# Routing logits of an attention-then-experts kernel: transposing the attention output on TensorE in fp32 instead of by DMA from DRAM in fp16

## The chip, the cores and the metric

The kernel runs on one core of one Trainium2 chip. The metric is device microseconds of that core, from the first to the last instruction and what lies around them, taken over whole executions; lower is better. The profile is one execution of the same program with the hardware profiler on.

## The reference: what is computed

Eight batches of eight heads go through attention (576 tokens, 64 columns a head). Four heads see a local band of 32 keys, four see the keys at a stride of 32. The output is laid out as 4608 tokens by 512 columns, and each token goes to one of eight experts, chosen greedily by the gate logits with a capacity of 576 tokens an expert.

```python
scores = scale * np.matmul(q, k.transpose(0, 1, 3, 2))
scores = np.where(masks[None, :, :, :], scores, -1000000000.0)
attn = softmax(scores)                       # 1e-09 added to the sum
x = np.matmul(attn, v).transpose(0, 2, 1, 3).reshape(B * S, H * D)
logits = x @ w_gate                          # 4608 x 8
...                                          # greedy assignment, cap tokens an expert
out[mask] = np.maximum(x[mask] @ w1[e], 0.0) @ w2[e]
```

The routing compares logits exactly, so the gates have to be as good as fp32.

## The kernel before, in words

**Units, pairs and steps.** The attention stage works on 16 units: for each batch `b` first its four strided heads (unit 2b, names with an `s`: `qs`, `ks`, `v_s`, `xs`), then its four local heads (unit 2b+1, names with an `l`). A unit is done in two pairs of heads, so there are 32 pairs, and a loop over steps `i` runs them in a pipeline that is written out by hand (`tc.manual_schedule()`): each engine takes its instructions in the order of the code, and none is moved. In step `i` stand, in this order, the second half of the scores of pair i+1 (`close_scores`: `dots` at L349, then the maximum on VectorE, L353), the first half of `mix` of pair i (L393, probabilities by values), the work of `mids`, the maximum of pair i+1 turned by TensorE and reduced (`max_t`, L359 to L367, ending in the tile `dd`), the second half of `mix`, the opening of the scores of pair i+2 (`masks` at L338 and the first `dots`), `norm` of pair i (L408 to L411, which writes the attention output `x` to SBUF), and `shift` of pair i+1 (L372 on TensorE, then the exponential on ScalarE, L376, which writes `pr`). Behind it come the fillers of that step (`fills`): the squares of the values on ScalarE (L288, for a common scale of each batch), `finish` (L423 on ScalarE and L424 on GpSimd split the fp32 output into two fp16 halves), `store` (DMAs to the scratch tensor `x_scr` in DRAM, L436 to L441) and `turn`. A batch is four steps.

**Memory.** The scores of a pair lie in a tile `spa` of two PSUM banks, of which there are two; `spb` is a tile of one bank, two again; `po` takes the two banks that are left. SyncE's queue issues, in the order of the code, the loads of `q`, `k` and `v` three units ahead, the stores, and the transposes; GpSimd's queue takes a part of the stores.

**The gates of before.** The two fp16 halves of a unit's output are read back from `x_scr` by a DMA that transposes them (`turn`, L446), two of these a batch. `gates` (L461) multiplies them with the gate weights, which `gate_weights`, `gate_scales` and `gate_parts` have split into two scaled fp16 halves as well (`wgh`): 16 fp16 matmuls a batch, each 32 columns wide, four side by side in the array, into 128 partial rows. ScalarE copies them to SBUF with the scale (`lt`, L464), and `logits` (L509) adds the partial rows and turns them to tokens with `sum_g`, five fp32 matmuls for each of the two layouts of a batch. Of the last batch, the local unit is turned on TensorE (`turn_last`, L477), split by ScalarE and VectorE (L485, L486), and `last_part` (L492) uses the output itself as stationary operand, 40 fp16 matmuls.

**Behind the attention.** VectorE takes the maximum of the logits, the routing search starts (L774), and the experts' stage follows: matmuls L1155 and L1203 with weights loaded and split as it goes. Nothing there is touched.

Shared helpers that the steps below rely on:

```python
def pair(i):
    return (todo[i // 2], i % 2) if 0 <= i <= last else None
def room(x):
    x[0].room(x[1])             # a new tile spa for the scores of this pair
    return x[0].sp[x[1]]
```

Of the kernel before, what the change touches and what calls it, by code (L numbers as in the profile page):

```python
# [21 lines left out]
STR = 32  # L22
# [110 lines left out]
def band_stride_attention_then_capacity_moe(ctx, tc, qt, kl, ks, nl, ns, wg, w1, w2, cst, out, dbg=None):  # L133
# [64 lines left out]
    def total(ss, po):  # L198
        nc.tensor.matmul(po, twos, ss, start=True, stop=True, skip_group_check=True)

# [19 lines left out]
    with tc.tile_pool(name="ld", bufs=2) as ld, \  # L220
# [24 lines left out]
        sg = None  # L245
        wgh = const.tile([128, H // 2, 4, E], F16, name="wgh")
        nc.vector.memset(wgh[:, :, 2:], 0.0)

        sqw = const.tile([128, 1], F32, name="sqw")
        jkw = wk.tile([128, H // 2, E], F16, name="jkw")  # L250

        def gate_weights(po):
            total(sqw, po[:, 0:1])
            nc.vector.tensor_copy(sqw, po[:, 0:1])

        def gate_scales():
            nonlocal sg
            sg, _ = scale_of(sqw, V_BITS, const)

        def gate_parts():  # L260
            nc.scalar.activation(wgh[:, :, 0], wg_sb, AF.Copy, scale=sg[:, 0:1])
            nc.vector.scalar_tensor_tensor(wgh[:, :, 1], wg_sb, sg[:, 0:1], wgh[:, :, 0], op0=OP.mult,
                                           op1=OP.subtract)

        class Unit:
# [177 lines left out]
            def turn(u):  # L443
                j = 1 if u.strided else 0
                u.xt = wk.tile([128, 2, 2, S], F16, name="xt" + u.g)
                nc.sync.dma_start_transpose(u.xt.rearrange("p a d n -> p (a d) n"), x_scr[u.b * S:(u.b + 1) * S, j])  # L446

        HB = S // 2
        ltb, gs = {}, {}

        def gate_scale(b):
            gs[b] = wk.tile([128, 1], F32, name="st")
            nc.vector.tensor_scalar(gs[b], vscale[b][0][:, 1:2], sg[:, 1:2], None, op0=OP.mult)

        def gates(b, po):
            lt = ltb[b] = wk.tile([128, S], F32, name="lt")
            xts = (todo[2 * b + 1].xt, todo[2 * b].xt)
            for a in range(2):
                for j in range(2):
                    for k in range(4):  # L460
                        nc.tensor.matmul(po[32 * k:32 * k + 32, j, :HB], wgh[:, k].rearrange("p a e -> p (a e)"),  # L461
                                         xts[k // 2][:, a, k % 2, j * HB:(j + 1) * HB],
                                         start=(a == 0), stop=(a == 1), skip_group_check=True)
            nc.scalar.activation(lt.rearrange("e (j n) -> e j n", j=2), po[:, :, :HB], AF.Copy, scale=gs[b])  # L464

        last_x = {}
# [4 lines left out]
        def turn_last(d, h, pt):  # L471
            u = todo[-1]
            j0, j1 = u.slots(parts[h])
            for j in range(j0, j1):
                n = min(128, S - 128 * j)
                x = u.x[:n, j, 2 * d:2 * d + 2].rearrange("q h d -> q (h d)")
                nc.tensor.transpose(pt[h][:, 128 * (j - j0):128 * (j - j0) + n], x, ident[:n, :n])  # L477
            if h == 0:
                last_x[d] = wk.tile([128, 2, S], F16, name=f"xtl{d}", bufs=1)

        def part_last(d, h, pt):
            c = span_l[h]
            n = c.stop - c.start
            xh, xl = (last_x[d][:, a, c] for a in range(2))
            nc.scalar.activation(xh, pt[h][:, :n], AF.Copy)  # L485
            nc.vector.scalar_tensor_tensor(xl, pt[h][:, :n], 1.0, xh, op0=OP.mult, op1=OP.subtract)  # L486

        def last_part(po, j, d):
            for a in range(2):
                for k, (r, _, tok) in enumerate(spans(B - 1)):  # L490
                    x = todo[2 * B - 2].xt[:, a, d, tok] if j else last_x[d][:, a, tok]
                    nc.tensor.matmul(po[r, k, :E * (2 - a)], x, wgh[:, 2 * j + d, :2 - a].rearrange("p a e -> p (a e)"),  # L492
                                     start=(j == 0 and d == 0 and k == 0 and a == 0), stop=(j == 1 and d == 1),
                                     skip_group_check=True)

        def last_gates(po):
            st = gs[B - 1]
            part = wk.tile([TP, 5, E], F32, name="lpart")
            sp = spans(B - 1)
            for r, c, k in ((sp[0][0], sp[0][1], slice(0, 4)), (sp[4][0], sp[4][1], slice(4, 5))):  # L500
                n = k.stop - k.start
                nc.vector.tensor_scalar(part[r, k], po[r, k, E:], st[r], None, op0=OP.mult)
                nc.vector.scalar_tensor_tensor(L[r, c:c + n], po[r, k, :E], st[r], part[r, k], op0=OP.mult, op1=OP.add)
# [26 lines left out]
        drips, late = {GW_AT + 1: [gate_scales]}, {GW_AT + 1: [gate_parts]}  # L530

        mids2, mids3 = {1: todo[1]}, {GW_AT: [lambda a, b: gate_weights(b)]}
        mids = {}

        for j, u in enumerate(todo):
# [16 lines left out]
            if not u.strided and u.b < B - 1:  # L552
                at(2 * j + (4 if u.b < B - 2 else 3), lambda k=u.b: gate_scale(k))
                if u.b < B - 2:
                    mids.setdefault(2 * j + (7 if u.b < B_LATE else G5), []).append(lambda a, b, k=u.b: gates(k, a))
                (mids if u.b == B - 2 else mids3).setdefault(2 * j + (L_AT if u.b < B_LATE else G5 + 1 if u.b < B - 2 else 5), []).append(lambda a, b, k=u.b: logits(k, b))
# [3 lines left out]
            if u is not todo[-1]:  # L560
                at(2 * j + (4 if j < 2 * B_LATE else 3 if j < nu - 2 else 1), u.turn)
# [14 lines left out]
        def pair(i):  # L576
            return (todo[i // 2], i % 2) if 0 <= i <= last else None
# [27 lines left out]
        for i in range(-1, 2 * nu):  # L605
# [17 lines left out]
            if i < last:  # L623
                for f in mids.get(i, []):
                    f(a, b)
            if i == last:
                gate_scale(B - 1)
# [15 lines left out]
            if i == last - 1:  # L643
                gates(B - 2, ps_a.tile([128, 2, 512], F32, name="spa"))
# [19 lines left out]
            if i == 0:  # L664
                nc.scalar.activation(jkw, wg_sb, AF.Square, accum_out=sqw)
            for f in late.get(i, []) + fills.get(i, []):
                f()
        po = ps_b.tile([128, 512], F32, name="spb")[:, :5 * 2 * E].rearrange("q (c e) -> q c e", e=2 * E)
# [10 lines left out]
        last_part(po, 0, 0)  # L679
        for h in range(2):  # L680
            part_last(1, h, pt)
        for f in summit(2, edge, (B - 1) * S // TP):
            f()
        for f in fills.get(last, []):
            f()
        last_part(po, 0, 1)
        for d in range(2):
            last_part(po, 1, d)
# [638 lines left out]
```

## Time and profile before

| what | value |
|---|---|
| time, median of 3 runs (lowest, highest) | 738.61 us (734.17, 739.92) |
| the profiled execution | 732.86 us, span 731.1 us |
| TensorE busy, all of the span | 622.4 us, 85% |
| VectorE, ScalarE, GpSimd busy | 456.3, 320.2, 154.1 us |
| attention, up to the last logits | 0 to 241 us |
| mean granted TensorE clock | 0.871 |

In the profile's slices, one digit is the tenths of a fortieth of the span. Rows of the timeline give the start, the duration, the engine, the source line, the operation with the tiles it writes and reads, and in brackets the idle time of the engine before it with what ended that. PE is TensorE, PEld its loading of stationary operands, DVE VectorE, ACT ScalarE, POOL GpSimd, SPq the issue queue of SyncE. "issue" in the brackets says that the profile shows nothing that was waited for. A tile written as `128*54 128x54` has 128 rows by 54 columns of stationary operand first and the moving operand behind it.

### The profile page before, as it was taken

The page shows a single profiled execution, that of the slowest core. Times are in us where ns is not written, and L with a number is a line of the kernel's source. Part 1 is how long each engine was busy: PE and PEld are TensorE (multiplying, and loading weights), DVE is VectorE, ACT ScalarE, POOL GpSimd, SP SyncE. Part 2 cuts the span into 40 slices and gives each one's busy share as a digit, 9 for nine tenths or more (in the row PEclk, how much of TensorE's full clock was granted, in tenths as well). Part 3 has the DMA queues.
Part 4 walks back from the last instruction along what each step waited for, and adds up shares of the span by engine and source line. Part 5 has one row for each costly group of instructions (what it writes and reads, how often), then busy time and mean ns, then how long its engine had stood idle before and what let it go on. Part 6 is the DMA issues. An engine that isn't in the chain of part 4 may idle for free.

```text
span 731.1 us, 19141 instructions
## 1 busy us (share of the span) xinstructions
PE 622.4 (85%) x8043; PEld 410.6 (56%) x8043; DVE 456.3 (62%) x1368; ACT 320.2 (44%) x497; POOL 154.1 (21%) x152
## 2 busy tenths in 40 slices
PE   6878886875889348999999997998998997999993
PEld 3656664654667326645845743754754753665741
DVE  3686666754787777887677674776766763652200
ACT  3444334435252024757166273356347345853210
POOL 2043223133133011032032032015005014212011
PEclk8575657878696557999999998999999999999998
DMA  9989999799764145076076087067068069561010
GB/s 217 247 244 251 215 237 202 210 238 173 212 133 97 36 159 160 1 281 146 1 281 144 1 288 139 1 229 183 16 218 207 1 222 254 211 114 51 1 37 29
DMA packets 106873, 111.23 MB, mean 152 GB/s; under 512 B 75644, under 2 KB 83414, under 8 KB 106275
## 3 DMA queue, kind: packets, MB, share of 16 engines
q1 hardware_dynamic: 98707, 88.46, 47.4%
q0 software_dynamic: 7360, 21.15, 9.5%
q8 instruction: 63, 1.03, 0.6%
q10 hardware_dynamic: 720, 0.39, 0.2%
q14 instruction: 23, 0.19, 0.1%
HBM read 73.60 MB, written 18.87 MB: 126 GB/s over the span
## 4 chain that ended last, share of the span: by engine, by line
PE 21%; DMA 14%; issue 13%; DVE 8%; SPq 4%; ACT 2%; POOL 2%; POOLq 0%; ACTq 0%; DVEq 0%
PE ph L1155 16%; DMA w<-in_w_dram 8%; DMA xg<-x_scr,idx 3%; SPq L1071 3%; PE ph L1203 3%; DMA xt<-xg 2%; DVE w2l L1017 2%; SPq L983 1%; POOL out_dram L1214 1%; ACT jk L998 1%; DVE hl L1163 1%; POOL xg L1068 1%; DVE cm L774 1%; ACT yl L1210 0%; DVE y L1211 0%
## 5 line engine op out<-in xcount | busy, mean ns | idle before, releaser
L1155 PE MATMUL ph<-xt,w1h 128*128 128x288 f16 (+2 forms) x1024 | 179.8, 291 | 13.0 <-DMA xt<-xg 9.4
L1155 PEld LDWEIGHTS <-w1h 128*128 128x128 f16 x1024 | 98.6, 99 | 44.2 <-issue 9.2
L1214 POOL DMA_INDIRECT out_dram<-y,idx x40 | 43.6, 1091 | 342.2 <-ACT y L1213 314.4
L1155 PE MATMUL ph<-xt,w1l 128*128 128x288 f16 (+2 forms) x512 | 113.9, 292 | 0.0
L998 ACT ACTIVATE jk<-w 128x1024 f16<-128x1024 f32 x64 | 67.5, 1054 | 75.1 <-DMA w<-in_w_dram 73.2
L1203 PE MATMUL ph<-w2h,hh 128*128 128x512 f16 x256 | 97.0, 379 | 0.0
L1203 PE MATMUL ph<-w2h,hl 128*128 128x512 f16 x256 | 97.0, 379 | 0.0
L1203 PE MATMUL ph<-w2l,hh 128*128 128x512 f16 x256 | 97.0, 379 | 0.0
L1162 ACT ACTIVATE hh<-ph 128x576 f16<-128x576 f32 (+2 forms) x72 | 42.9, 596 | 120.3 <-PE ph L1155 117.6
L1203 PEld LDWEIGHTS <-hh 128*128 128x128 f16 x512 | 48.4, 98 | 59.6 <-issue 9.7
L1163 DVE SCALAR_TENSOR_TENSOR hl<-ph,hh 128x576 f16<-128x576 f32 (+2 forms) x72 | 49.5, 688 | 42.2 <-ACT hh L1162 41.9
L376 ACT ACTIVATE pr<-spa 128x576 f32<-128x576 f32 x32 | 20.8, 650 | 110.3 <-PE spa L372 92.9
L1155 PEld LDWEIGHTS <-w1l 128*128 128x128 f16 x512 | 50.6, 100 | 13.8 <-issue 0.8
L424 POOL TENSOR_TENSOR xos<-xs,xos 118x768 f16<-118x768 f32 x16 | 26.7, 1672 | 122.8 <-ACT xos L423 122.8
L1068 POOL DMA_INDIRECT xg<-x_scr,idx x40 | 41.6, 1039 | 49.0 <-issue 34.7
L1017 DVE SCALAR_TENSOR_TENSOR w1l<-w,w_sw,w1h 128x512 f16<-128x512 f32 x64 | 45.8, 747 | 9.1 <-ACT w1h L1016 3.9
L1017 DVE SCALAR_TENSOR_TENSOR w2l<-w,w_sw,w2h 128x512 f16<-128x512 f32 x64 | 45.8, 745 | 7.9 <-ACT w2h L1016 7.8
L393 PE MATMUL po<-v_s,pr 64*54 64x65 f32 (+1 forms) x768 | 42.7, 268 | 7.2 <-issue 4.7
L1213 ACT ACTIVATE y<-ph,so 128x512 f32<-128x512 f32 x32 | 21.9, 683 | 57.4 <-PE ph L1203 37.8
L1016 ACT ACTIVATE w1h<-w,w_sw 128x512 f16<-128x512 f32 x64 | 41.7, 709 | 3.2 <-DVE ss_e L203 1.8
L1016 ACT ACTIVATE w2h<-w,w_sw 128x512 f16<-128x512 f32 x64 | 41.1, 710 | 3.7 <-DVE w_sw L208 3.6
L1203 PEld LDWEIGHTS <-hl 128*128 128x128 f16 x256 | 25.0, 98 | 29.4 <-issue 3.6
(613 smaller groups left out, 972.6 us busy)
## 6 DMA issues: line engine op xcount, KB each, us to landing
w<-in_w_dram SPq DMA_DIRECT2D x64, 512.0 KB
v_s<-in_ns_dram SPq DMA_DIRECT2D x16, 329.1 KB
kl<-in_kl_dram SPq DMA_DIRECT2D x8, 608.0 KB
v_l<-in_nl_dram SPq DMA_DIRECT2D x16, 292.5 KB
ql<-in_qt_dram SPq DMA_DIRECT2D x8, 576.0 KB
x_scr<-xol SPq DMA_DIRECT2D x8, 512.0 KB
ks<-in_ks_dram SPq DMA_DIRECT2D x7, 576.0 KB
qs<-in_qt_dram SPq DMA_DIRECT2D x7, 576.0 KB
```

What stands on the lines that cost most here:

```text
L393: nc.tensor.matmul(po[r:r + n, j - j0], pr[k, o:o + n], u.vn[k, t, 2 * p + h], start=(j == j0), stop=(j == j1 - 1), skip_group_check=True)
L424: eng.tensor_tensor(u.xo[:nr, :, 1, c], xf, u.xo[:nr, :, 0, c], op=OP.subtract)
L998: nc.scalar.activation(jk, wf[:, c * n4:(c + 1) * n4].rearrange("p c f -> p (c f)"), AF.Square, scale=1.41422, accum_out=sq[:, c:c + 1])
L1016: nc.scalar.activation(hi[:, c, f], wf[:, c, f], AF.Copy, scale=s_)
L1017: nc.vector.scalar_tensor_tensor(lo[:, c, f], wf[:, c, f], s_, hi[:, c, f], op0=OP.mult, op1=OP.subtract)
L1068: nc.gpsimd.indirect_dma_start(out=xg[:n], out_offset=None, in_=x_rows, in_offset=bass.IndirectOffsetOnAxis(ap=idx[:n, t:t + 1], axis=0))
L1071: nc.sync.dma_start_transpose(xt[:, :, t * 128:t * 128 + n], xg[:n])
L1155: nc.tensor.matmul(tile_[:, j, :w], wt[:, d, f * 128:(f + 1) * 128], xt[:, d // 2, xx, d % 2, c], start=(k == 0), stop=(k == 3 * DC - 1))
L1162: nc.scalar.activation(hv, src, AF.Relu)
L1163: nc.vector.scalar_tensor_tensor(lv, src, 0.0, hv, op0=OP.max, op1=OP.subtract)
L1203: nc.tensor.matmul(py, a[:, f, ts_], w[:, f], start=(k == 0), stop=(k == len(todo) - 1))
L1214: st = nc.gpsimd.indirect_dma_start(out=out_rows, out_offset=bass.IndirectOffsetOnAxis(ap=idx[:n, t:t + 1], axis=0), in_=y[:n], in_offset= ...
```

## The change

No DMA transposes are left in the attention. Each pair's output, which lies in SBUF in fp32, is transposed on TensorE one step after it was made (`turn(p, po)`): 12 transposes of a strided pair, 6 of a local one. They are written into the PSUM tile `a` that the scores of pair i+2 will take later in the same step, and ScalarE copies them to SBUF (`keep`) before those scores are opened. The first strided pair has its own path (`turn_first`, at the end of step 2). The gate weights stay in fp32, padded to 32 columns with zeros (`wgp`), and `gates(b, j)` is called twice a batch, as a filler of two successive steps: four fp32 matmuls each, of 288 columns, side by side in the array. The strided half of `lt` is written in the order of the tokens, by an activation of its own. The scales of the gate weights and their three functions go. Of the last batch, `last_strided` and `last_part` do the same in fp32, with 15 matmuls in place of 40. `finish` and `store` stay, because the experts read `x_scr`.

```diff
-            def turn(u):
-                j = 1 if u.strided else 0
-                u.xt = wk.tile([128, 2, 2, S], F16, name="xt" + u.g)
-                nc.sync.dma_start_transpose(u.xt.rearrange("p a d n -> p (a d) n"), x_scr[u.b * S:(u.b + 1) * S, j])
+            def turn(u, p, po):
+                if u.b not in xtb:
+                    xtb[u.b] = wk.tile([128, H // 2, S], F32, name="xt")
+                for j, c, t, r in u.pieces():
+                    x = u.x[r, t, 2 * p:2 * p + 2].rearrange("q h d -> q (h d)")
+                    nc.tensor.transpose(po[:, j, c:c + r.stop - r.start], x, ident[r, r])
+
+            def pieces(u):
+                if u.strided:
+                    return [(f, SQ * t, t, slice(64 * f, 64 * f + u.wide(t))) for t in range(u.nt) for f in range(2)]
+                return [(0, EV + 128 * j, j, slice(0, 128)) for j in range(3)] + \
+                    [(1, 128 * (j - 2), j, slice(0, min(128, S - 128 * j))) for j in range(2, u.nx)]
+
+            def keep(u, p, po):
+                o = 0 if u.strided else EV
+                nc.scalar.activation(xtb[u.b][:, 2 * u.strided + p].rearrange("d (j n) -> d j n", j=2), po[:, :, o:o + HB],
+                                     AF.Copy)
...
-        def gates(b, po):
-            lt = ltb[b] = wk.tile([128, S], F32, name="lt")
-            xts = (todo[2 * b + 1].xt, todo[2 * b].xt)
-            for a in range(2):
-                for j in range(2):
-                    for k in range(4):
-                        nc.tensor.matmul(po[32 * k:32 * k + 32, j, :HB], wgh[:, k].rearrange("p a e -> p (a e)"),
-                                         xts[k // 2][:, a, k % 2, j * HB:(j + 1) * HB],
-                                         start=(a == 0), stop=(a == 1), skip_group_check=True)
-            nc.scalar.activation(lt.rearrange("e (j n) -> e j n", j=2), po[:, :, :HB], AF.Copy, scale=gs[b])
+        def lt_parts(lt, po, sc, js):
+            for j, c in js:
+                nc.scalar.activation(lt[64:].rearrange("e (a r) -> e a r", r=STR)[:, :, 16 * j:16 * j + 16],
+                                     po[64:, c].rearrange("e (r a) -> e a r", a=NA), AF.Copy, scale=sc)
+
+        def gates(b, j):
+            if j == 0:
+                ltb[b] = wk.tile([128, S], F32, name="lt")
+            lt, c = ltb[b], slice(64, 64 + HB)
+            po = ps_b.tile([128, 512], F32, name="spb")
+            for k in range(4):
+                nc.tensor.matmul(po[32 * k:32 * k + 32, c], wgp[:, k], xtb[b][:, k, j * HB:(j + 1) * HB], start=True,
+                                 stop=True, skip_group_check=True)
+            sc = vscale[b][0][:, 1:2]
+            nc.scalar.activation(lt[:64, j * HB:(j + 1) * HB], po[:64, c], AF.Copy, scale=sc[:64])
+            lt_parts(lt, po, sc[64:], [(j, c)])
...
             if not u.strided and u.b < B - 1:
-                at(2 * j + (4 if u.b < B - 2 else 3), lambda k=u.b: gate_scale(k))
-                if u.b < B - 2:
-                    mids.setdefault(2 * j + (7 if u.b < B_LATE else G5), []).append(lambda a, b, k=u.b: gates(k, a))
+                for h in range(2):
+                    at(2 * j + 3 + h, lambda k=u.b, h=h: gates(k, h))
...
-            if u is not todo[-1]:
-                at(2 * j + (4 if j < 2 * B_LATE else 3 if j < nu - 2 else 1), u.turn)
...
                 for f in mids.get(i, []):
                     f(a, b)
+                if i > 1:
+                    x = pair(i - 1)
+                    po = a if m else ps_a.tile([128, 2, 512], F32, name="spa")
+                    x[0].turn(x[1], po)
+                    x[0].keep(x[1], po)
             if i == last:
-                gate_scale(B - 1)
+                last_strided()
...
-            if i == last - 1:
-                gates(B - 2, ps_a.tile([128, 2, 512], F32, name="spa"))
...
+            if i == 2:
+                for j in range(2):
+                    todo[0].turn_first(j)
```

**The order on TensorE.** One step of a middle batch on PE, from the last `dots` of the next pair to the `masks` of the one behind it (`mix` of a strided unit is L393 here, `max_t` L359), before:

```order
L349 MATMUL spa<-qs,ks 54x54 x16
L349 MATMUL spa<-qs,ks 18x18 x4
L393 MATMUL po<-v_s_129,pr 54x65 x10
L393 MATMUL po<-v_s_129,pr 18x65 x2
L359 MATMUL spa<-ident,mx_s_131 32x64 x4
L393 MATMUL po<-v_s_129,pr 54x65 x10
L393 MATMUL po<-v_s_129,pr 18x65 x2
L338 LDWEIGHTS ident_b
L338 MATMUL spa<-mask_l,ident_b 128x288
```

The same step in the changed kernel, whose lines are numbered 20 lower up to here (L329 is the `dots`, L373 `mix`, L339 `max_t`, L318 the `masks`; L428 is the new transpose):

```order
L329 MATMUL spa<-qs,ks 54x54 x16
L329 MATMUL spa<-qs,ks 18x18 x4
L373 MATMUL po<-v_s_129,pr 54x65 x10
L373 MATMUL po<-v_s_129,pr 18x65 x2
L428 MATMUL spa<-ident,xl 128x128 x5
L428 MATMUL spa<-ident,xl 128x64
L339 MATMUL spa<-ident,mx_s_131 32x64 x4
L373 MATMUL po<-v_s_129,pr 54x65 x10
L373 MATMUL po<-v_s_129,pr 18x65 x2
L318 LDWEIGHTS ident_b
L318 MATMUL spa<-mask_l,ident_b 128x288
```

The transposes of the pair before (a local one, `xl`) stand between the first half of `mix` and `max_t`; the `masks` write the tile that the transposes went into.

**The order on ScalarE.** Two steps of a middle batch on ACT before, from one exponential to the third (`jk` are the squares of the values, `xos` and `xol` are `finish`):

```order
L376 ACTIVATE pr<-spa 128x576
L288 ACTIVATE jk,vsq_115<-v_l_141 32x2304
L423 ACTIVATE xos<-xs 118x6x128
L376 ACTIVATE pr<-spa 128x576
L288 ACTIVATE jk,vsq_115<-v_l_141 32x2304
L423 ACTIVATE xol<-xl 128x5x128
L376 ACTIVATE pr<-spa 128x576
```

The first of them in the changed kernel, to the next exponential (L438 is `keep`, L467 and L455 write `lt`, L356 is the exponential, L268 the squares, L403 `finish`):

```order
L356 ACTIVATE pr<-spa 128x576
L268 ACTIVATE jk,vsq_115<-v_l_141 32x2304
L467 ACTIVATE lt<-spb,ss_s 64x288
L455 ACTIVATE lt<-spb,ss_s 64x18x16
L403 ACTIVATE xos<-xs 118x6x128
L438 ACTIVATE xt<-spa 128x576
L356 ACTIVATE pr<-spa 128x576
```

Between two exponentials now stand `keep` in every step and the two `lt` activations in two steps of four.

**The order on SyncE.** A batch's worth of the SP queue before; the changed kernel has the same rows without the two marked DMA_TRANSPOSE, and nothing else of the queue moves:

```order
L446 DMA_TRANSPOSE xts<-x_scr 128x4x576
L440 DMA x_scr<-xol 128x4x512
L441 DMA x_scr<-xol 64x512
L319 DMA v_s_133<-in_ns_dram 54x1560 x2
L312 DMA ks<-in_ks_dram 128x1152
L313 DMA qs<-in_qt_dram 128x1152
L446 DMA_TRANSPOSE xtl<-x_scr 128x4x576
L436 DMA x_scr<-xos 18x6x512
```

Each transpose stands behind loads of later units and ahead of stores and loads that the queue issues in turn.

More of the change, by code (lines that the diff above doesn't have):

```diff
@@ L243, in band_stride_attention_then_capacity_moe @@
                 vbuf[g, i] = t
[L245 to L263, printed above, removed]
+        wgp = const.tile([128, H // 2, 32], F32, name="wgp")
+        nc.vector.memset(wgp, 0.0)
         class Unit:
@@ new lines, in keep, with turn_first @@
+            def keep(u, p, po):
+                o = 0 if u.strided else EV
+                nc.scalar.activation(xtb[u.b][:, 2 * u.strided + p].rearrange("d (j n) -> d j n", j=2), po[:, :, o:o + HB],
+                                     AF.Copy)
+            def turn_first(u, j):
+                po = ps_b.tile([128, 512], F32, name="spb")
+                for f, c, t, r in u.pieces():
+                    if f == j:
+                        nc.tensor.transpose(po[:, c:c + r.stop - r.start], u.x[r, t, :2].rearrange("q h d -> q (h d)"),
+                                            ident[r, r])
+                nc.scalar.activation(xtb[u.b][:, 2, j * HB:(j + 1) * HB], po[:, :HB], AF.Copy)
@@ L488, in last_part @@
[L488 to L493, printed above, removed]
+            x = xtb[B - 1][:, d, c]
+            if h == 0:
+                nc.scalar.activation(x, pt[h][:, :c.stop - c.start], AF.Copy)
+            else:
+                nc.vector.tensor_copy(x, pt[h][:, :c.stop - c.start])
@@ new lines, in last_strided @@
+        def last_strided():
+            lt = ltb[B - 1] = wk.tile([128, S], F32, name="lt")
+            po = ps_a.tile([128, 2, 512], F32, name="spa")
+            for j in range(2):
+                for k in range(2, 4):
+                    nc.tensor.matmul(po[32 * k:32 * k + 32, j, :HB], wgp[:, k], xtb[B - 1][:, k, j * HB:(j + 1) * HB],
+                                     start=True, stop=True, skip_group_check=True)
+            for j in range(2):
+                lt_parts(lt, po[:, j], 1.0, [(j, slice(0, HB))])
@@ L494, in last_part @@
+        def last_part(po, k, first):
+            for n, (r, _, tok) in enumerate(spans(B - 1)):
+                if k is None:
+                    nc.tensor.matmul(po[r, n], ltb[B - 1][64:, tok], sum_g[64:], start=False, stop=False,
+                                     skip_group_check=True)
+                else:
+                    nc.tensor.matmul(po[r, n], xtb[B - 1][:, k, tok], wgp[:, k, :E], start=(first and n == 0), stop=(k == 1),
                                      skip_group_check=True)
@@ L496, in last_gates @@
         def last_gates(po):
-            st = gs[B - 1]
-            part = wk.tile([TP, 5, E], F32, name="lpart")
+            st = vscale[B - 1][0][:, 1:2]
             sp = spans(B - 1)
@@ L663, in band_stride_attention_then_capacity_moe @@
                 todo[1].square_v(i + 1)
-            if i == 0:
-                nc.scalar.activation(jkw, wg_sb, AF.Square, accum_out=sqw)
+            if i == 2:
+                for j in range(2):
+                    todo[0].turn_first(j)
             for f in late.get(i, []) + fills.get(i, []):
                 f()
-        po = ps_b.tile([128, 512], F32, name="spb")[:, :5 * 2 * E].rearrange("q (c e) -> q c e", e=2 * E)
+        po = ps_b.tile([128, 512], F32, name="spb")[:, :5 * E].rearrange("q (c e) -> q c e", e=E)
         turn_last(0, 0, pt)
@@ L685, in band_stride_attention_then_capacity_moe @@
             f()
-        last_part(po, 0, 1)
-        for d in range(2):
-            last_part(po, 1, d)
+        last_part(po, 1, False)
         last_gates(po)
```

28 lines of the change are left out of this document (9 added, 19 removed).

## The prediction

> **What bounds the kernel now.** The change touches only the attention, so I cut the span there by batches: windows of four steps, from one exponential (L376) to the fourth behind it, in the view that gives each engine's busy time, the granted TensorE clock, the DMA share and the rate by window.
>
> ```profile
> 29.40:58.50 29.10, 21.79 (x540) 15.72 (x538) 24.00 (x60) 11.91 (x15) 9.90 (x8) 0.70 0.90 260
> 58.50:86.40 27.90, 23.07 (x550) 16.53 (x554) 18.00 (x48) 12.27 (x16) 8.19 (x7) 0.68 0.98 233
> 86.40:114.20 27.80, 24.56 (x564) 18.52 (x565) 18.59 (x48) 12.17 (x15) 8.12 (x7) 0.65 0.96 224
> 114.20:142.30 28.10, 20.50 (x568) 15.35 (x572) 18.07 (x49) 12.21 (x16) 7.92 (x7) 0.76 0.89 210
> 142.30:172.00 29.70, 22.75 (x568) 16.36 (x563) 17.75 (x49) 12.14 (x16) 8.20 (x7) 0.77 0.95 206
> 172.00:201.80 29.80, 21.46 (x568) 15.72 (x564) 18.16 (x51) 12.16 (x16) 7.93 (x7) 0.77 0.85 203
> 201.80:225.40 23.60, 21.17 (x573) 15.98 (x570) 20.54 (x54) 10.93 (x13) 8.35 (x7) 0.86 0.63 128
> ```
>
> The columns behind the length are PE, PEld, DVE, ACT, POOL, then clock, DMA share and GB/s. Five middle batches take 27.9 + 27.8 + 28.1 + 29.7 + 29.8 = 143.3 us, 28.7 each. DMA is 85 to 98% busy in them, TensorE 72 to 88%. The batch behind them has the same work on TensorE, but the last load was issued before it and DMA is at 63%: 23.6 us.
>
> ```profile
> 190.96 1.38 SPq L313 DMA_DIRECT2D ql<-in_qt_dram  x1
> ```
>
> So a middle batch loses some 5 us to the DMAs. The list of waits in these five batches says how:
>
> ```profile
> PE spa L349 <- issue: 12.7, 3, 6.4
> PE spa L359 <- issue: 6.0, 2, 3.8
> PE spa L372 <- DVE dd L367: 4.4, 4, 1.3
> PE po L393 <- issue: 3.6, 3, 2.0
> PE spa L461 <- issue: 2.1, 1, 2.1
> ```
>
> 12.7 + 6.0 + 3.6 + 2.1 = 24.4 us of TensorE's idle time have no releaser that the profile shows. No data is missing: in the timeline the pause falls inside a run of like matmuls. The longest two:
>
> ```profile
> 113.83 8.98 SPq L446 DMA_TRANSPOSE xtl<-x_scr  x1
> 119.16 0.65 ACT L376 ACTIVATE pr<-spa 128x576 f32<-128x576 f32 x1 [1.16 <-PE spa L372]
> 124.82 0.45 PE L349 MATMUL spa<-qs,ks 64*54 64x54 f32 x8 [5.70 <-issue]
> ...
> 172.24 9.34 SPq L446 DMA_TRANSPOSE xtl<-x_scr  x1
> 183.97 0.26 PE L349 MATMUL spa<-qs,ks 64*18 64x18 f32 x6 [6.41 <-issue]
> ```
>
> They end 2.0 and 2.4 us after the transpose has left the SP queue (122.81 and 181.58). The DMA queues by window, first while the transpose is being moved (113.9 to 122.2 us), then at its end (122.2 to 124.8):
>
> ```profile
> q1 hardware_dynamic: 1223, 1.86, 102.5%
> ```
>
> ```profile
> q8 instruction: 1, 0.02, 2.5%
> ```
>
> A 16 KB block of instructions comes through only when the transpose is over. I read the pauses as TensorE out of instructions, whose fetch stands behind the transposes in the DMA engines. [...]
>
> **The change part by part.** *Removed:* 15 DMA transposes, two a batch; with them, by my reading, most of the 24.4 us.
>
> *Added on TensorE:* the transposes of 30 pairs, one pair a step. The prices, from the timeline at full clock:
>
> ```profile
> 234.33 0.86 PE L477 MATMUL spa<-ident,xl 128*128 128x128 f32 x5
> 235.12 0.44 PE L477 MATMUL po<-ident,xl 128*128 128x128 f32 x2
> ...
> 110.64 1.00 PE L393 MATMUL po<-v_s,pr 64*54 64x65 f32 x24
> ...
> 233.13 1.27 PE L509 MATMUL spb<-sum_g,lt 128*128 128x8 f32 x10
> ...
> 115.96 0.32 PE L359 MATMUL spa<-ident,mx_l 128*32 128x64 f32 x8
> ...
> 229.24 0.30 PE L461 MATMUL spa<-xtl,wgh 128*32 128x288 f16 x2
> 229.62 0.29 PE L461 MATMUL spa<-xts,wgh 128*32 128x288 f16 x2
> ```
>
> A local pair: five such transposes stand 0.79 us from the next group (234.33 to 235.12), one more makes 0.90. A strided pair has 12 of 54 rows by 128 columns, which no row shows: as cheap as `mix`, which also alternates between the two halves of the rows, 12 x 1.00/24 = 0.5; as dear as L509, which loads 128 fp32 columns each time, 12 x 1.27/10 = 1.5. I take 0.9, near the middle, since it shares one trait with each. A batch: 4 x 0.9 = 3.6 us. The fp32 gates: eight matmuls of 288 columns, four side by side. L359 ran eight of 64 columns, also in fours, in 0.32, of which about 0.2 is one matmul's own way; the second four thus cost 0.1, or 0.46 for 288 columns; two calls with their starts 1.1 (not side by side, it would be 3.7). The 16 fp16 matmuls that go took 0.67 (229.24 to 229.91). Net +0.4, so 4.0 us a batch at full clock, 4.0/0.86 = 4.7 at the clock of the undisturbed batch.
>
> *Added on ScalarE:* `keep` in each step, two pairs of `lt` activations, less one `lt`.
>
> ```profile
> L464 ACT ACTIVATE lt<-spa,st x7: 731/741/742, 80.2 to 230.0; 128x576 f32<-128x576 f32 x7
> L288 ACT ACTIVATE jk<-v_l x16: 2118/2121/2124, 16.3 to 207.4; 32x2304 f16<-32x2304 f32 x16
> L423 ACT ACTIVATE xos<-xs x16: 826/838/844, 40.5 to 226.0; 118x768 f16<-118x768 f32 x16
> ```
>
> ```profile
> 234.81 0.44 ACT L485 ACTIVATE xtl<-spa 128x320 f16<-128x320 f32 x1 [2.94 <-PE spa L477]
> ```
>
> `keep` has the shape of L464, 0.74; the `lt` pieces are a little shorter than L485, 0.4 each. ScalarE is free for more than half of a batch (12.2 of 28), but `keep` is waited for: the `masks` write the tile that it reads, and behind them stand on TensorE the opening `dots`, the second `shift` and with it the next exponential. In the two steps of a batch with local squares the queue is 0.65 + 2.12 + 0.18 + 0.8 + 0.84 + 0.74 = 5.3 us from an exponential to the end of `keep`, and masks, dots and shift about 1.5 more: 6.9 us a step. The step I forecast is 28.7/4 = 7.2, so the wait is mostly covered; at full clock it shows. I put 0.7 us a batch, between none and 2.
>
> *Given back:* the wait for `dd` (4.4 us in five batches) is on VectorE, which is behind with copies; a turn now stands ahead of `max_t` and fills it: -0.9 a batch. *Left:* fetches behind plain loads, 0.6 a batch, an estimate from the short pauses in the list.
>
> *The sum.* A middle batch: 23.6 + 4.7 + 0.7 - 0.9 + 0.6 = 28.7, five of them 143.5 against 143.3: +0.2. The batch of 201.8 to 225.4 has no pause to win back: +4.7 - 0.9 = +3.8. The window 29.4 to 58.5 lies almost wholly before the first transposes (53.6 on): four turns, the first unit's own and less weight work, 4.1/0.70 = 5.9, less a wait that hides 3.0 of it:
>
> ```profile
> L446 SPq DMA_TRANSPOSE xts<-x_scr x8: 2139/4069/6582, 53.6 to 233.9; - x8
> ```
>
> ```profile
> 50.77 0.64 PE L372 MATMUL spa<-dd,sel 128*128 128x288 bf16 x2 [2.99 <-DVE dd L367]
> ```
>
> That is +2.9. At the end:
>
> ```profile
> 236.24 1.60 PE L492 MATMUL spb<-wgh,xtl 128*128 128x16 f16 x20 [0.68 <-ACT xtl L485]
> 238.44 1.48 PE L492 MATMUL spb<-wgh,xts 128*128 128x16 f16 x20 [0.59 <-DMA xts<-x_scr]
> 240.78 0.23 DVE L503 SCALAR_TENSOR_TENSOR L<-spb,st,lpart 64x8 f32<-64x8 f32 x1
> ```
>
> Of 40 matmuls, 15 of 0.127 stay, and only five of them behind the last copies, which no longer follow each other on ScalarE and VectorE: the last transposes end at 235.6 (235.12 + 0.44), a copy 0.5, five matmuls 0.6, two writes of the logits 0.5, some 0.3 between them: near 237.5, not 241.0, -3.5; one more turn and `last_strided` cost (0.9 + 1.1 - 0.1)/0.8 = +2.3. Together -1.2. In all +0.2 + 3.8 + 2.9 - 1.2 = **+5.7 us**. The experts' stage keeps its order and shifts. The profiled execution took 732.86 us (span 731.1), so 738.6; the median of the runs, 738.61, is 5.75 above it, and on that the forecast is 744.3 us, 0.8% more. A measurement of this kernel can tell about 1% from no change.
>
> **The rivals.** *The clock stays low (slower).* I priced the added work at 0.86; in the middle batches it was granted at 0.65 to 0.77. Busy time by clock gives 15.7, 16.0, 15.6, 17.5 and 16.5 us of work a batch at full clock, 16.3 in the mean; with 4.0, at 0.73, 27.8 us, and with the idle of the last batch (23.6 - 21.2 = 2.4) and 0.4 more 30.6: +9.7 in place of +0.2, and +5 in place of +3.8: 755. For it: 86.4 to 114.2 has short pauses and still 0.65. Against: the pauses of 4 to 6 us fall into half-clock stretches. A stretch with ten transposes ran at full clock, the next at half:
>
> ```profile
> 232.29:235.71 3.42, 3.27 (x42) 2.43 (x31) 2.33 (x9) 0.44 (x1) 1.47 (x4) 1.00 0.14 37
> 235.71:239.12 3.41, 2.25 (x30) 1.87 (x30) 2.89 (x8) 1.61 (x4) 1.40 (x1) 0.50 0.72 163
> ```
>
> [...]
>
> *ScalarE's loop decides (slower).* If `keep` ends 1.5 us late in both steps with local squares, each batch pays 3.0 and not 0.7: +11.5, 756. It decides once TensorE's step is under 6.9 us.
>
> *The clock rises (faster).* Without pauses TensorE may be near full clock: at 0.92 the work is 22.1, and ScalarE's loop then sets two steps of four: 2 x 6.9 + 2 x (22.1 + 2.4)/4 = 26.0 a batch, -13.5, and -1.8 in the batch behind: 729.
>
> *The pauses are not the transposes'.* The loads share the engines; then the 24.4 us stay, each middle batch pays 4.7 + 0.7 - 0.9 = 4.5, +22.5 in place of +0.2: 767. Against it: the pauses end with the transposes. That transposes remain is excluded by the order of SP.
>
> **How the numbers follow.** The forecast, 744, own range 738 to 751: 0.35. Clock low, 755: 0.22. ScalarE, 756: 0.12. Pauses stay, 767: 0.06. Clock rises, 729: 0.25. Faster by over 1% is the last, 0.25; within 1% the forecast, 0.35; slower 0.40. From 724 to 762 leaves out most of the fourth and the far ends of the clock cases, under 0.2.
>
> **What would show it.** Right: DMA share near 0.7 in the middle batches, TensorE's pauses without releaser under 5 us in all, L428 at 0.9 us a turn, middle batches of 28 to 29 us, the batch behind them 27 to 28, logits done 3 us sooner after the last exponential. Wrong: pauses of 4 us that remain; L428 over 1.5 a strided turn; `masks` waiting for `keep` over 1 us in most steps; a mean clock under 0.7 or over 0.9 up to 225 us.

## The result and the profile after

The changed kernel takes 747.05 us (median of 19 runs, 737.89 to 754.43), the kernel before 736.48 us (19 runs, 726.58 to 741.58): ratio 1.0151, 95% interval 1.0112 to 1.0190. In this ratio and those below, executions over 1.5% above the fastest of their kernel are left out; the medians hold all. The profiled execution took 744.54 us with a span of 742.8, against 732.86 and 731.1. The forecast was 744.3 us, 0.8% slower: the side was right and the time lies in the stated range, though the change of +10.6 us is nearly twice the +5.7 forecast. The place was wrong: the forecast put its 5.7 us into the attention, and the profile has none there.

The windows of four steps for the kernel after, from exponential (now L356) to exponential, cut as in the prediction (columns: length, PE, PEld, DVE, ACT, POOL, clock, DMA share, GB/s):

```profile
30.90:64.50 33.60, 27.40 (x582) 20.59 (x586) 22.85 (x54) 15.27 (x21) 9.86 (x8) 0.70 0.73 215
64.50:91.60 27.10, 22.44 (x596) 16.09 (x597) 19.92 (x48) 16.02 (x22) 7.95 (x7) 0.94 0.65 184
91.60:117.90 26.30, 22.35 (x596) 16.22 (x598) 20.08 (x48) 16.06 (x22) 8.12 (x7) 0.94 0.66 187
117.90:147.20 29.30, 23.21 (x596) 16.64 (x597) 19.74 (x48) 16.02 (x23) 7.94 (x7) 0.88 0.60 169
147.20:173.10 25.90, 21.96 (x596) 15.58 (x592) 19.03 (x48) 15.91 (x22) 8.25 (x7) 0.93 0.68 190
173.10:199.40 26.30, 22.41 (x596) 16.52 (x598) 20.40 (x49) 16.05 (x23) 7.94 (x7) 0.94 0.63 180
199.40:224.50 25.10, 20.58 (x596) 15.17 (x592) 20.51 (x52) 14.53 (x20) 7.95 (x7) 1.00 0.18 50
```

The five middle batches take 134.9 us in place of 143.3, though TensorE has more to do: the granted clock is 0.88 to 0.94 where it was 0.65 to 0.77, and DMA is busy for two thirds of the time and not for nearly all. Busy time by clock is 20.8 us a batch at full clock (21.1, 21.0, 20.4, 20.4, 21.1) against 16.3 before: 4.5 more, where the prediction added 4.0. What TensorE waits for in these five batches (64.5 to 199.4 us; columns: total us, times, longest):

```profile
PE spa L318 <- ACT xt L438: 11.3, 9, 1.9
PE spa L352 <- DVE dd L347: 6.8, 9, 1.0
PE spa L329 <- issue: 3.1, 3, 2.6
PE po L373 <- ACT pr L356: 0.7, 4, 0.2
PE spb L519 <- issue: 0.6, 1, 0.6
```

Pauses without a releaser are 3.7 us in place of 24.4. In their stead `masks` (L318) wait for `keep` (L438). One step of ScalarE's queue shows why, with the `masks` behind it:

```profile
98.31 0.65 ACT L356 ACTIVATE pr<-spa 128x576 f32<-128x576 f32 x1 [1.20 <-PE spa L352]
...
98.98 2.12 ACT L268 ACTIVATE jk<-v_l 32x2304 f16<-32x2304 f32 x1
...
101.22 0.50 ACT L467 ACTIVATE lt<-spb,ss_s 64x288 f32<-64x288 f32 x1
...
101.73 0.50 ACT L455 ACTIVATE lt<-spb,ss_s 64x288 f32<-64x288 f32 x1
...
102.25 0.74 ACT L403 ACTIVATE xol<-xl 128x640 f16<-128x640 f32 x1
...
103.01 0.65 ACT L438 ACTIVATE xt<-spa 128x576 f32<-128x576 f32 x1
...
103.71 0.41 PE L318 MATMUL spa<-mask_s,ident_b 128*128 128x288 bf16 x2 [0.34 <-ACT xt L438]
```

From the exponential to the end of `keep` it is 103.66 - 98.31 = 5.35 us, the 5.3 of the prediction.

Over the whole attention the gain of the middle is given back at its edges. From the first exponential's window to the start of the search: start +1.5 (third exponential at 30.91, before at 29.37), first window +4.5, middle -8.4, the batch behind +1.6, last step and logits +0.5. The search starts at 245.35 us; before it started at 245.67. **In this pair of executions all 11.7 us of the span arise behind it**, where the change touches no line. (A profile is one execution, and the attention of the changed kernel is not always this short: in the profiles of two runs below, `after_less32` and `after_again`, the search starts at 253.0 and 254.8 us. What the attention costs is therefore taken from the cuts and ratios below.) First the kernel before from the search to the end, its window, its longest wait on the gathered tokens' transposes, and its queue of gathers and scatters (packets, MB, share of 16 engines):

```profile
245.70:731.10 485.40, 433.00 (x3550) 273.57 (x3550) 295.35 (x927) 220.44 (x369) 85.32 (x81) 0.94 0.44 127
```

```profile
PE ph L1155 <- DMA xt<-xg: 9.4, 6, 2.2
```

```profile
q0 software_dynamic: 5888, 18.88, 12.9%
```

The same three of the kernel after:

```profile
245.40:742.80 497.40, 436.67 (x3550) 274.62 (x3550) 295.53 (x927) 221.01 (x369) 85.61 (x81) 0.94 0.45 124
```

```profile
PE ph L1165 <- DMA xt<-xg: 15.6, 10, 2.9
```

```profile
q0 software_dynamic: 5888, 18.88, 13.5%
```

The counts of instructions, the packets and bytes of these queues and the clock are the same, but it takes 12.0 us more. The experts' hidden matmuls wait 6.2 us longer for the transposed tokens, and the same 5888 packets take 13.5% of a longer span, 67.1 us in place of 62.6 on each of 16 engines. Comparing the two built programs, one thing differs in this stage beside the DMAs' semaphore lanes and the place of the instructions in memory: every SBUF tile behind the attention lies 32 bytes a partition higher, since the new `wgp` and what it replaces do not have the same size. The first expert weights `w1` begin at byte 59616 before and 59648 after.

### The profile page after: what moved, and what is told of

The parts are those of the page before. It is cut to its first block, busy times and chain, and to the rows that moved or that the text cites. A ratio compares the mean times of both kernels' runs of the same rounds, so it can differ in the third digit from the quotient of the medians.

```text
span 742.8 us, 19700 instructions
## 1 busy us (share of the span) xinstructions
PE 634.2 (85%) x8315; PEld 416.5 (56%) x8315; DVE 464.5 (63%) x1351; ACT 348.7 (47%) x546; POOL 153.8 (21%) x152
## 4 chain that ended last, share of the span: by engine, by line
PE 19%; DMA 16%; issue 13%; DVE 6%; POOL 4%; ACT 2%; SPq 2%; POOLq 0%; ACTq 0%
PE ph L1165 17%; DMA w<-in_w_dram 8%; DMA xg<-x_scr,idx 6%; DMA xt<-xg 3%; POOL xg L1078 2%; POOL out_dram L1224 1%; DVE w2l L1027 1%; ACT jk L1008 1%; SPq L993 1%; DVE hl L1173 1%; SPq L1081 1%; DVE y L1221 0%; ACT yl L1220 0%; DVE cm L830 0%; PE ph L1066 0%
## 5 line engine op out<-in xcount | busy, mean ns | idle before, releaser
L1165 PE MATMUL ph<-xt,w1h 128*128 128x288 f16 (+2 forms) x1024 | 183.2, 296 | 19.7 <-DMA xt<-xg 15.6
L356 ACT ACTIVATE pr<-spa 128x576 f32<-128x576 f32 x32 | 20.8, 651 | 72.6 <-PE spa L352 72.6
L404 POOL TENSOR_TENSOR xos<-xs,xos 118x768 f16<-118x768 f32 x16 | 26.4, 1653 | 128.2 <-ACT xos L403 128.2
L373 PE MATMUL po<-v_s,pr 64*54 64x65 f32 (+1 forms) x768 | 35.7, 238 | 6.9 <-ACT pr L356 6.7
```

Source lines behind the costliest of these rows:

```text
L373: nc.tensor.matmul(po[r:r + n, j - j0], pr[k, o:o + n], u.vn[k, t, 2 * p + h], start=(j == j0), stop=(j == j1 - 1), skip_group_check=True)
L404: eng.tensor_tensor(u.xo[:nr, :, 1, c], xf, u.xo[:nr, :, 0, c], op=OP.subtract)
L1165: nc.tensor.matmul(tile_[:, j, :w], wt[:, d, f * 128:(f + 1) * 128], xt[:, d // 2, xx, d % 2, c], start=(k == 0), stop=(k == 3 * DC - 1))
```

## The experiments

Theory A: the cost arises in the attention, as predicted (the change pays there, the experts shift). Theory B: it arises behind the attention. Two kernels are cut behind the logits; routing and experts are left out, so what they write is not the reference's output.

```diff
+    nc.sync.dma_start(out[0:TP, 0:NC * E], L.rearrange("q c e -> q (c e)"))
+    return
```

`attn_before`:

> The kernel of before that ends behind the attention: it writes the logits into the first 128 rows of the output and leaves the routing and the experts out. Its profile before has the logits done at 241 us, so a time near 247 us. It is the base for the next one. Theory A (the change costs its 11 us in the attention, and the profiled execution was a lucky one) expects it 8 to 12 us under attn_after; theory B (the 11 us arise behind the attention) expects the two within 3 us.

`attn_after`:

> The changed kernel cut in the same way (no routing, no experts). Theory A: 255 to 259 us, 8 to 12 more than attn_before. Theory B: within 3 us of attn_before, near 246 us, since the profiled execution of the changed kernel had its last exponential at 230.0 us against 230.6.

Measured: 248.56 us (247.72 to 249.28, 4 runs) and 249.41 us (246.93, 249.28, 249.55, 271.45). The attention costs 0.9 us more by the medians, and 0.1 by the means without the run of 271.45 (248.6 against 248.5); theory A falls. For B, the address was moved alone, once in each kernel.

`before_pad32` gives the kernel before the addresses of the change behind the attention:

```diff
+        pad = const.tile([128, 8], F32, name="pad")
+        nc.vector.memset(pad, 0.0)
```

> The kernel of before with 32 bytes a partition of unused constants more, so that every tile of the routing and of the experts lies at the address that it has in the changed kernel. If the addresses of the SBUF tiles are what makes the experts' stage of the changed kernel longer: 9 to 12 us over the kernel before (1.012 to 1.016). If not: the ratio to before is within 0.4% of 1.

`after_less32` gives the changed kernel those of before:

```diff
-        warm_e = const.tile([128, 1], F32, name="warm_e")
+        warm_e = rm0[:, :1]
```

> The changed kernel with 32 bytes a partition less in front of the experts' tiles (a scratch word of the warm-up activation lies in another tile), so that these lie where they lie in the kernel before. If the addresses are the cause: within 0.4% of the kernel before. If not: 1.011 to 1.019 times the kernel before, as the changed kernel.

Measured: 739.46 us, ratio 1.0044 (0.9994 to 1.0093), and 738.85 us, ratio 1.0029 (0.9982 to 1.0077). So 32 bytes less take the changed kernel back to the kernel before, but 32 more hardly slow the kernel before, where 1.012 to 1.016 was expected of the address. To exclude that only the session had changed, the change was run again, beside a sibling 32 bytes *higher* (the two lines of `pad` ahead of `wgp`):

> The changed kernel, unaltered, measured again beside its shifted sibling. Address theory (the experts' stage is slower because all tiles behind the attention lie 32 bytes higher): 1.2 to 1.8% above the kernel before, search to end 494 to 500 us. Rival (the 10 us belonged to the first comparison or to the chip, not to the kernel): within 0.5% of before.

> The changed kernel with a constant of 32 bytes a partition more, so that the tiles behind the attention lie another 32 bytes higher: 64 above those of the kernel before, again an odd multiple of 32. Address theory, if what counts is whether a base is an odd or an even multiple of 32 bytes: within 0.5% of before, as with 32 bytes less. If any other property of the change slows the experts' stage: 1.2 to 1.8% above before, like the unaltered change.

Measured: `after_again` 749.06 us, 1.0179 (1.0127 to 1.0231); `after_plus32` 734.71 us, 0.9995 (0.9962 to 1.0028). It is not height but place: 32 bytes either way remove the loss. Next the shift was confined to what follows the attention, in both kernels:

```diff
+    pd = ctx.enter_context(tc.tile_pool(name="pd", bufs=1))
+    pad = pd.tile([128, 8], F32, name="pad")
+    nc.gpsimd.memset(pad, 0.0)
     rt = ctx.enter_context(tc.tile_pool(name="rt", bufs=2))
```

> The changed kernel with 32 bytes a partition put in between the attention and what follows: the attention's tiles stay where the change has them, only those of the routing and the experts lie 32 bytes higher. Theory that the address costs its time in the experts' stage: 0.995 to 1.006 of before, search to end 484 to 490 us. Rival that a part of it arises in the attention's own tiles: 1.006 to 1.012. Rival that it is another property: 1.015 to 1.018, 494 to 498 us.

> The kernel before with the same 32 bytes between the attention and what follows, so that the experts' tiles alone stand where the change has them. If the address is the whole cause: 1.008 to 1.018 of before, search to end 492 to 498 us. Rival (as the constant of 32 bytes in the kernel before hinted with 1.0044): 0.999 to 1.006, so the address costs its full price only together with something else that the change brings.

Measured: `after_rtpad` 740.21 us, 0.9980 (0.9935 to 1.0025): the attention's own tiles have no part in it. `before_rtpad` 741.10 us, 1.0011 (0.9966 to 1.0056): the rival holds, the address alone does not have its full price in the kernel before. All nine full kernels, sorted by where `w1` begins (the other tiles of the stage move by the same amount). The third column is from the profiled executions, search to end; then the wait of the hidden matmuls for `xt`, and the time of the 4608 packets of 4096 bytes on the queue of gathers and scatters, summed from the trace. Stage, wait and packets are of one execution each:

| kernel | `w1` at byte, rest by 256 | search to end, us | wait for `xt`, us | gather and scatter packets, engine-us | ratio to before |
|---|---|---|---|---|---|
| after | 59648, 0 | 497.4 | 15.6 | 1065 | 1.0151 |
| after_again | 59648, 0 | 495.0 | 15.9 | 1023 | 1.0179 |
| before_pad32 | 59648, 0 | 491.7 | 11.0 | 1013 | 1.0044 |
| before_rtpad | 59648, 0 | 490.4 | 11.9 | 1036 | 1.0011 |
| after_less32 | 59616, 224 | 488.8 | 7.2 | 983 | 1.0029 |
| before | 59616, 224 | 485.4 | 9.4 | 989 | 1 |
| after_rtpad | 59680, 32 | 485.2 | 4.7 | 980 | 0.9980 |
| after_plus32 | 59680, 32 | 485.0 | 11.4 | 992 | 0.9995 |
| both (below) | 59680, 32 | 481.2 | 9.2 | 966 | 1.0006 |

The row of the wait in `before_rtpad` and in `after_rtpad`, the two kernels that differ from their parents only in this:

```profile
PE ph L1158 <- DMA xt<-xg: 11.9, 8, 2.5
```

```profile
PE ph L1168 <- DMA xt<-xg: 4.7, 5, 1.6
```

All four with `w1` on a multiple of 256 have the longest stage and the slowest packets, whichever attention stands ahead; no kernel of the other five reaches them, though the nearest two are close (490.4 and 488.8 us). The three places that were tried do not tell a multiple of 256 from one of 64 or 128. In the changed kernel this is worth 11 us (496.2 against 485.1 in the mean of two and four), and the ratios say the same three times. In the kernel before it is worth 5.6 us in two profiles and 1 to 3 us in the medians of the runs, within what the intervals allow to be nothing. **That the loss is removed by moving the experts' tiles by 32 bytes is shown; why the address costs more behind the new attention is open**, as is which tile it is. At the change's addresses `w1`, the gathered tokens `xg` and their transposes `xt` all start on multiples of 256 bytes, and in the table the kernels with that place have the longer packets, 1013 to 1065 engine-us against 966 to 992. It is not the ordinary packet that differs: the median is 159 to 161 ns in all nine. Packets of more than 400 ns number 422 to 495 with `w1` on a multiple of 256 and 343 to 382 elsewhere; and the stage's 33792 packets of 256 bytes, those of the transposes, took 885 to 965 engine-us there and 811 to 880 elsewhere. What holds them up is open.

Inside the attention, three cuts test the terms of the sum. `attn_relief` is `attn_before` without its 15 DMA transposes; the gates read a tile of zeros, so the logits are left meaningless:

```diff
-                u.xt = wk.tile([128, 2, 2, S], F16, name="xt" + u.g)
-                nc.sync.dma_start_transpose(u.xt.rearrange("p a d n -> p (a d) n"), x_scr[u.b * S:(u.b + 1) * S, j])
+                u.xt = xt0
```

> The attention of the kernel before alone (cut behind the logits), without its 15 DMA transposes; the gates read a tile of zeros in their place, so the logits are not the reference's. Nothing is added on TensorE or ScalarE. Theory that TensorE's pauses come from the transposes: 222 to 228 us in place of 248.6, pauses without a releaser under 5 us in the five middle batches. Rival (the loads cause the pauses): 243 to 249.

Measured: 226.59 us (224.16 to 228.16, 4 runs), 22.0 less than `attn_before`. So the transposes cost 22 us, and the work that replaces them 249.4 - 226.6 = 22.8. (The cuts ran on three chips, on which the kernel before took 734.1 to 738.8 us; a difference of 1 to 2 us between cuts can be the chip.) Pauses without a releaser from 58 to 200 us, `attn_before` and then `attn_relief`:

```profile
PE spa L349 <- issue: 12.1, 4, 6.2
PE po L393 <- issue: 9.0, 5, 5.4
PE spa L359 <- issue: 5.8, 2, 4.7
PE spa L461 <- issue: 1.1, 1, 1.1
```

```profile
PE spa L351 <- issue: 8.1, 4, 3.7
PE po L395 <- issue: 5.8, 6, 2.8
...
PE spa L361 <- issue: 1.9, 1, 1.9
...
PE spa L462 <- issue: 0.6, 1, 0.6
```

28.0 us become 16.4, not the under 5 expected: the longest go, shorter ones stay with plain loads alone. The total was forecast well and this part of its reason was not; in the same window the granted clock rose from 0.71 to 0.84. (The windows of this cut hold more steps, since it is faster.) When the pauses end can be read from the traces: in `before`, `attn_before` and `attn_relief` each of the 18 pauses over 1.5 us in the middle batches ends 1.2 to 1.8 us after a 16 KB block has landed on the instruction queue, and the five waits of 1.9 us for `keep` in the changed kernel hold no such landing. That agrees with the prediction's reading, TensorE out of instructions; it stays a reading, since no run changes the fetch alone.

`attn_keep` moves the squares of the local values from behind the exponential to behind `keep`:

```diff
-                        at(2 * j - V_AT + f, lambda u=u, f=f: u.square_v(f), True)
+                        squares[2 * j - V_AT + f] = lambda u=u, f=f: u.square_v(f)
...
                     x[0].keep(x[1], po)
+                if i in squares:
+                    squares[i]()
```

> The attention of the changed kernel alone (cut behind the logits, routing and experts left out), with ScalarE's squares of the local values moved from behind the exponential to behind keep. Theory that the wait of masks for keep is what holds the loop (15.7 us in 12 waits): 236 to 241 us, in place of 249.4, and that wait under 4 us. Rival (the loop is held by TensorE's own work or by the DMAs, and the wait only shows slack): 246 to 250.

Measured: 246.65 us (241.39 to 257.05, 4 runs), 2.8 less and not 8 to 13; the expectation failed. The runs go with the granted clock; at like clocks the gain is 3.6 us (245.71 at 0.857 against 249.28 at 0.853) and 5.5 (241.39 at 0.879 against 246.93 at 0.877). TensorE's waits over the whole cut, `attn_after` and then `attn_keep`:

```profile
PE spa L318 <- ACT xt L438: 14.4, 11, 1.9
PE spa L352 <- DVE dd L347: 9.1, 11, 1.4
PE po L373 <- issue: 5.8, 3, 4.2
PE spa L329 <- issue: 3.3, 4, 2.1
```

```profile
PE spa L352 <- DVE dd L347: 16.7, 15, 3.3
PE spa L329 <- issue: 10.9, 6, 4.0
PE po L373 <- issue: 7.7, 4, 4.1
```

The wait for `keep` is gone, all 14.4 us, and 7.6 us of it came back as the wait for `dd`, 9.5 as pauses without a releaser. For `dd`, the timeline of `attn_keep` shows VectorE's small cast (L344) at seven times its length while GpSimd's subtraction of `finish` (L404) runs, and one without it:

```profile
141.90 1.65 POOL L404 TENSOR_TENSOR xos<-xs,xos 118x768 f16<-118x768 f32 x1 [6.32 <-ACT xos L403]
...
142.29 1.29 DVE L344 CAST mh<-mr 128x32 bf16<-128x32 f32 x1
...
157.86 0.18 DVE L344 CAST mh<-mr 128x32 bf16<-128x32 f32 x1
```

In these rows the long cast ends 0.03 us behind the subtraction (143.58 and 143.55). So do the others of this trace: 10 of its 25 casts from 59 to 225 us take over 0.8 us, and each ends 0.03 to 0.04 us behind a subtraction. The change made this worse without touching either line: the same cast from 59 to 225 us in the kernel before, and then in `attn_after` (count, busy us, mean ns):

```profile
L364 DVE CAST mh<-mr 128x32 bf16<-128x32 f32 x24 | 5.0, 208 | 0.8
```

```profile
L344 DVE CAST mh<-mr 128x32 bf16<-128x32 f32 x25 | 13.2, 529 | 0.9
```

`attn_keep2` moves `finish` behind the squares as well, out of the cast's way:

```diff
-                at(2 * j + p if j else 2, lambda u=u, p=p: u.finish(p, nc.gpsimd))
+                if 0 < j < nu - 2:
+                    fin[2 * j + p + 1] = lambda u=u, p=p: u.finish(p, nc.gpsimd)
+                else:
+                    at(2 * j + p if j else 2, lambda u=u, p=p: u.finish(p, nc.gpsimd))
...
+                if i in fin:
+                    fin[i]()
```

> The attention of the changed kernel alone, with the squares of the local values behind keep and with finish (ScalarE's copy, GpSimd's subtraction) behind both. Theory that the wait for dd, which took the place of the wait for keep (16.7 us in 15 waits), comes from VectorE's small cast L344, 0.18 us alone and 1.2 to 1.3 while GpSimd's subtraction runs: mean of L344 in 59 to 225 us from 614 to under 300 ns, that wait under 9 us, 238 to 243 us. Rival (VectorE's queue itself is late, or TensorE's pauses decide): 245 to 250 with the wait as long.

The cast in 59 to 225 us, and the waits of the cut:

```profile
L344 DVE CAST mh<-mr 128x32 bf16<-128x32 f32 x25 | 4.5, 181 | 0.9
```

```profile
PE po L373 <- issue: 8.7, 4, 5.5
PE spa L329 <- issue: 8.2, 3, 3.2
PE po L373 <- ACT pr L356: 6.3, 9, 1.1
PE spa L352 <- DVE dd L347: 5.6, 3, 3.2
```

The cast and the wait came out as expected, 181 ns and 5.6 us; the time is 245.75 us (244.19 to 247.06, 4 runs), in the rival's range and not in the 238 to 243. What is left over stands as pauses without a releaser (16.9 us) and as waits for the exponential (6.3); that TensorE, with less idle time, comes sooner to the end of its instructions and to `pr` is a reading and not tested.

Last, `both`: the whole changed kernel with 32 bytes more (as `after_plus32`) and with ScalarE's order of `attn_keep2`.

> The whole changed kernel with 32 bytes a partition more in its constants, and with the squares and finish behind keep on ScalarE. If the gains add: 0.9995 from the 32 bytes, less the 3.7 us of the attention alone (249.4 to 245.8), 0.990 to 0.999 of before, so level with or a little ahead of both kernels; search to end 484 to 490 us. Rival: the order of ScalarE brings nothing in the whole kernel, or the experts' stage answers again to what stands ahead of it: 1.000 to 1.015.

Measured: 730.57 us (726.32 to 736.37, 12 runs), ratio 1.0006 (0.9968 to 1.0045) to the kernel before, 732.75 us in these runs. The rival holds: it wins back what the change lost and no more: against `after_plus32` (0.9995) ScalarE's order brings nothing that can be measured; the 3.7 us expected would be 0.5%, little more than these intervals can tell. No version here beats the kernel before.

## Why the prediction was right in its time and wrong in its place

*"With them, by my reading, most of the 24.4 us."* Right for the change: 3.7 us are left in the middle batches. Too narrow as a cause: without transposes and with nothing in their place 16.4 us stay in 142 us, the longest 3.7 against 6.2 with them. And in the change a part is only covered: from 58 to 200 us `attn_after` has 3.4 us of pauses, `attn_keep`, without the wait for `keep`, 12.6.

*Turns at 0.9 us, gates at net +0.4.* Near, by errors that cancel. A strided and a local turn of a middle batch:

```profile
60.48 0.68 PE L428 MATMUL spa<-ident,xs 54*128 54x54 f32 x12
...
74.65 0.97 PE L428 MATMUL spa<-ident,xl 128*128 128x128 f32 x6
```

The local turn stands 0.90 us from the next group (74.65 to 75.55), as forecast, the strided one 0.61 (60.48 to 61.09), a third less. From 30 to 230 us the 29 turns were busy for 26.1 us, 0.90 each, at a granted clock of 0.90. The gates of the seven batches took 11.4 us, 1.6 a batch, and those that they replace 6.3, or 0.9: net +0.7. The work that the sum added, 4.0 us a batch at full clock, came out at 4.5.

*"4.0/0.86 = 4.7 at the clock of the undisturbed batch."* This term failed. The clock went to 0.88 to 0.94 as the pauses left; that was the rival "the clock rises" (0.25), which put the middle at 26.0 us a batch. Three batches took 25.9 to 26.3, one 27.1, one with the last long pause 29.3. In place of +0.2 the middle brought -8.4 in this execution. (The rival's 729 adds its -1.8 for the batch behind to the forecast's +3.8; with the one in place of the other its terms give 725.) The middle batches have 3.3 to 3.9 us of the new transposes each, and the clock rose with them in place.

*"I put 0.7 us a batch, between none and 2"* for `keep`. Too low: 11.3/5 = 2.3, above the upper bound, because the loop of 6.9 us that the prediction worked out met a TensorE faster than the 7.2 it assumed. Yet the runs show that this wait has little price of its own: without its 14.4 us, 2.8 are gained by the medians and 3.6 to 5.5 at like clocks.

*"-0.9 a batch"* for `dd`. Wrong sign: 6.8 us in place of 4.4. The turn does stand ahead of `max_t`, but the cast now meets GpSimd's subtraction (617 ns each in the profile after, from 59 to 225 us, against 208 before).

*The edges.* Expected +2.9, +3.8, -1.2; measured +4.5, +1.6, and +2.1 for the logits (the start, +1.5, had no term), which end 12.5 us after the last exponential (242.58 - 230.04) and not 10.4 (241.01 - 230.60). The prediction counted the entries of the trace as matmuls. The fp32 matmuls of the logits are two entries each (the five of a `logits` call are listed as x10), so behind the last copies stand ten entries and not five, and the ten of the strided half stand ahead of them, all at 0.21 us each where the granted clock was 0.52 (237.7 to 242.1 us), in place of the 0.127 measured at 1.00:

```profile
237.79 2.13 PE L502 MATMUL spb<-sum_g,lt 64*128 64x8 f32 x10
...
239.86 2.19 PE L505 MATMUL spb<-wgp,xt 128*128 128x8 f32 x10
...
242.08 0.50 DVE L513 TENSOR_SCALAR L<-spb,ss_s 128x32 f32<-128x32 f32 x2 [3.00 <-PE spb L505]
...
244.47 0.38 POOL L723 PARTITION_ALL_REDUCE rng<-pk  x1 [5.87 <-DVE oh L196]
```

It cost nothing, since GpSimd's reduction of the peak, which the search waits for, came no later. In all nine full kernels this reduction stands 5.8 to 6.1 us behind GpSimd's instruction before it (here the last subtraction of `finish`) and 1.4 to 3.8 us behind the peak; so within these margins the end of the logits, for which the prediction had a term, does not set the start of the search. What fills the 6 us the profile does not show. Before, it stood here:

```profile
241.35 0.16 DVE L711 TENSOR_REDUCE pk<-peak 128x1 f32<-128x5 f32 x1
...
244.79 0.38 POOL L713 PARTITION_ALL_REDUCE rng<-pk  x1 [5.90 <-issue]
```

*"The experts' stage keeps its order and shifts."* The step that failed. The order was kept, the shift was -0.3 us, and the stage itself took 12.0 us longer. Nothing in the profile of before can price this. That the time still came out in the stated range is luck: an attention that turned out even (+0.9 alone) and an experts' stage some 11 us longer at its address give +10.6 where +5.7 was forecast. With the tiles elsewhere the change measures 0.998 to 1.003: of no effect that these runs can tell.

*"What would show it."* Of the signs of being right, the DMA share (0.60 to 0.68), the pauses (3.7 us) and the price of a turn (0.90) came true; the middle batches (25.9 to 29.3 us for 28 to 29), the batch behind them (25.1 for 27 to 28) and the logits did not.

## What to carry to other kernels

When a change leaves a stage untouched, compare that stage's span in both profiles before explaining anything in the stage that was edited; cutting both kernels behind the edited stage shows where the time goes. A difference in an untouched stage can come from the place of its tiles (11 us of 497 here, 1.5 and 1.8% of the kernel's time): shift them by a few bytes (32 here) in both directions, on both kernels, before the edit is blamed or praised. And a wait that shows 14 us in a list is not 14 us of time: remove it once and see which wait takes its place.

## What was not expected of the hardware

The attention of the changed kernel goes with the granted clock of the single run. `attn_after` took 246.9 us at a mean clock of 0.877, 249.3 at 0.853 and 249.6 at 0.851, and one run of 271.5 at 0.734; `attn_keep` 241.4 at 0.879, 245.7 at 0.857, 247.6 at 0.840 and 257.1 at 0.798. `attn_before` took 247.7 to 249.3 at 0.746 to 0.753. In the profiles of `after`, `after_plus32`, `after_less32` and `after_again` the search starts at 245.4, 245.5, 253.0 and 254.8 us, in the three with the old attention at 242.1 to 245.7. So the edit may also have traded a steady time for one that varies; four runs of a cut and one profile of a kernel hint at it and do not show it.

The other surprise is the address: 32 bytes a partition, in either direction, decide over 11 us of 497 in a stage whose instructions, packets and bytes are the same. The runs show where it is paid (hidden matmuls waiting for transposed tokens, gather and scatter packets 2 to 10% longer in sum, by more of the long ones), and that in the kernel before the same address costs less than the runs can tell. They do not show the mechanism.
